# Block-sparse attention with a gated projection: the factor 0.125 moves from the queries to the maxima and the exponential

## The chip, the cores and the metric

The kernel runs on one core of one Trainium2 chip. The metric is device time in microseconds (us) of that core, the median of the runs. The engines are PE (TensorE: matmuls; PEld is its weight load), DVE (VectorE), ACT (ScalarE), POOL (GpSimd) and SP (SyncE, which here only issues DMAs). Each works through its own instructions in order; semaphores join them.

## The reference

What is computed, cut to what matters (batch B = 4, H = 8 heads, S = 768 rows, D = 64; blocks of 32 rows, 24 of them):

```python
scale = 1.0 / np.sqrt(D)                                  # 0.125
scores = scale * np.matmul(q, k.transpose(0, 1, 3, 2))
scores = np.where(mask, scores, -1000000000.0)
scores = scores - np.max(scores, axis=-1, keepdims=True)
attn = np.exp(scores)
attn = attn / (np.sum(attn, axis=-1, keepdims=True) + 1e-09)
x = np.matmul(attn, v)                                    # heads side by side: (B, S, 512)
gate = sigmoid(sum over k of conv_w[k] * x shifted by 4 - k rows)
out = (gate * (x @ w_val)) @ w_out
```

The mask lets a block see itself and its two neighbours, the first and the last block, and three sampled blocks; the first and last block see all and are seen by all. All data are fp32.

## The kernel before

The work goes in units. A *pair unit* is two neighbouring blocks of queries (64 rows) over all eight heads: each of its blocks has eight blocks of keys, 256 columns. A *global unit* holds queries of the first or last block, which see all 768 columns. Each batch has 11 pair units and 2 global ones, and there are 52 units in all. The 128 partitions of a score tile are 4 head pairs x 32 rows; the two heads of a head pair have a tile each, which is why most things happen twice per unit ("both heads").

For a unit, `scores` (from line 330) lets PE write the scores to PSUM (`sc`, three banks; `s` for global units). For each head DVE then takes the negated maxima (`mx`, line 365 for pairs: one reduce gives both blocks' maxima, 128 x 2). ACT takes the exponentials with the maximum as bias (`pe`, lines 367 and 368; `rest` and `first` in global units, lines 350 and 351). In a global unit two reduces per head give two partial maxima, and a small `tensor_tensor` joins them (line 348).

`transposes` turns the exponentials on PE (`pt`) and ACT copies them back to SBUF (`ptr`). `values` multiplies with the values (`av`); DVE forms the reciprocal of the sums (`rs`) and scales (`x`). `finish` transposes `x` into `xT`. Behind the attention comes the gated projection in rows of up to 384: DVE's convolution (`th`), ACT's splits (`xh`, `yh`), POOL's remainders (`xl`, `yl`), DVE's product (`y`) and two projections on PE (`vp`, `op`). In the first third DVE also decodes the two weight matrices from 64-bit words (`words`, `wst`, `wv`, `wo`).

The order on each engine is the order in which the program is written; the class `InOrder` (line 59) fixes it and is the reason why nearly every instruction has line 65 in the profile. The main loop (line 622) goes over steps n. In a step it issues the loads, the scores of unit n, the copies of keys (`kg`, on POOL and ACT in the first two batches, POOL and DMA later), the values of unit n - 2, the transposes of unit n - 1, and between them pieces of the projection (`fill`) and of decoding or gating (`prepare`).

Queries arrive by DMA in `qc` (128 x 256, five buffers). Before a unit's scores, `scale` (line 616) multiplies them in place by 0.125, two units ahead (`SCALE_AHEAD`): on ACT in batches 0 and 1, on DVE in batches 2 and 3, 24 times each.

Of the kernel before, what the change touches and what calls it, by code (L numbers as in the profile page):

```python
# [11 lines left out]
AF = mybir.ActivationFunctionType  # L12
ALU = mybir.AluOpType
# [19 lines left out]
LAG_T, LAG_V = 1, 2  # L33
WEIGHTS_AT = (1, 3, 5, 7, 9, 10, 11, 13)
DECODE_LAG = 2
SCALE_AHEAD = 2
COPY_AHEAD = 2

COPIED = [{0: POOL, 1: POOL, 2: POOL, 3: ACT, 4: ACT, 5: ACT}] * 2 + [{}] * 2
# [7 lines left out]
def attention_moe(ctx, tc, qb, kb, v, sampled, w_val, conv_w, w_out, ident_in, slot_in, out):  # L47
# [29 lines left out]
    pe, dve, act, pool, sp = (InOrder(e) for e in (nc.tensor, nc.vector, nc.scalar, nc.gpsimd, nc.sync))  # L77
# [45 lines left out]
    for r in range(NR):  # L123
# [3 lines left out]
            out=base[rows, :], in0=sf[rows, r, :], scalar1=float(BLK), scalar2=off[rows], op0=ALU.mult, op1=ALU.add  # L127
# [3 lines left out]
    def indices(b):  # L131

        row = const.tile([128, NB], F32, tag=f"row{b % 2}", name="row")
        dve.tensor_scalar_add(row, base, float(b * S - B * S))
        dve.tensor_tensor(out=row, in0=row, in1=valid, op=ALU.mult)
        dve.tensor_scalar_add(idx[:, b, :], row, float(B * S))
# [100 lines left out]
    for bt in batches:  # L237
        for p in [*range(GLOB_AFTER + 1), -1, *range(GLOB_AFTER + 1, NP - 1)]:
            pr = Pair()
# [4 lines left out]
    def block_numbers(pr, eng):  # L244

        mine = [n for n in range(2 * NR) if COPIED[pr.bt.b].get(n, SP) == eng]
        if not mine:
            return
        first = NR * PAIRS[pr.p][0] + mine[0]
        _, regs = nc.values_load_multi_w_load_instructions(  # L250
            sm[0:1, first : first + len(mine)], engines=[eng], min_val=0, max_val=NB - 1,
            skip_runtime_bounds_check_because="block numbers are drawn from [0, 24)",
        )
        for n, reg in zip(mine, regs):
            yield 5 + 4 * (n // NR) + n % NR, reg
# [69 lines left out]
    def heads():  # L325
        for hp in range(HP):
            for h in range(2):
                yield hp, h, slice(64 * h, 64 * h + 64), slice(BLK * hp, BLK * hp + BLK)

    def scores(un):  # L330
        pr = un.pr
        un.P = []
        if pr.glob:
            lo = [ps_sc.tile([128, 512], F32, tag="sc", name="s0") for _ in range(2)]
            hi = [space.tile([128, 512], F32, tag=tag, name="s1") for space, tag in ((ps_sc, "sc"), (ps_pt, "pt"))]
            for k0 in range(3):
                for hp, h, rows, cols in heads():
                    dst = hi[h][cols, 0:256] if k0 == 2 else lo[h][cols, 256 * k0 : 256 * k0 + 256]
                    matmul(
                        dst, pr.qc[rows, hp, un.e, :], pr.bt.k[rows, 8 * k0 : 8 * k0 + 8, cols],  # L340
                        start=True, stop=True, tile_position=(64 * h, BLK * hp),
                    )
            mx = three.tile([128, 2, 4], F32, tag="mx", name="mx")
            rest = five.tile([128, 2, 256], F32, tag="pr", name="rest")
            for h in range(2):
                dve.tensor_reduce(out=mx[:, h, 0:1], in_=lo[h], axis=AX.X, op=ALU.max, negate=True)
                dve.tensor_reduce(out=mx[:, h, 1:2], in_=hi[h][:, 0:256], axis=AX.X, op=ALU.max, negate=True)
                dve.tensor_tensor(out=mx[:, h, 2:3], in0=mx[:, h, 0:1], in1=mx[:, h, 1:2], op=ALU.min)
                first = five.tile([128, 512], F32, tag="pr", name="first")
                act.activation(rest[:, h, :], hi[h][:, 0:256], AF.Exp, bias=mx[:, h, 2:3])  # L350
                act.activation(first, lo[h], AF.Exp, bias=mx[:, h, 2:3])
                un.P.append(first)
            un.P.append(rest.rearrange("p h k -> p (h k)"))
            return
        sc = [ps_sc.tile([128, 2, 256], F32, tag="sc", name="sc") for _ in range(2)]
        kt = pr.kg.rearrange("p (t e) x -> p t e x", e=4)
        for j in range(2):
            for hp, h, rows, cols in heads():
                matmul(
                    sc[h][cols, j, :], pr.qc[rows, hp, j, :], kt[rows, 0 : 2 + j : 1 + j, :, cols],  # L360
                    start=True, stop=True, tile_position=(64 * h, BLK * hp),
                )
        mx = three.tile([128, 2, 4], F32, tag="mx", name="mx")
        for h in range(2):
            dve.tensor_reduce(out=mx[:, h, 0:2], in_=sc[h], axis=AX.X, op=ALU.max, negate=True)
            pe_ = five.tile([128, 2, 256], F32, tag="pr", name="pe")
            for j in range(2):
                act.activation(pe_[:, j, :], sc[h][:, j, :], AF.Exp, bias=mx[:, h, j : j + 1])
            un.P.append(pe_.rearrange("p j k -> p (j k)"))

    def transposes(un):
        un.PT = []
        for p in un.P:
            pt = ps_pt.tile([128, 4, 128], F32, tag="pt", name="pt")
            for c in range(4):
                transpose(pt[:, c, :], p[:, 128 * c : 128 * c + 128], ident)
            t = three.tile([128, 4, 128], F32, tag="ptr", name="ptr")
            act.copy(t, pt)
            un.PT += [t[:, c, :] for c in range(4)]
            yield  # L380
# [169 lines left out]
    def store():  # L550
        while stores:
            sp.dma_start(*stores.pop(0))
# [42 lines left out]
            advance(to_split, prepared)  # L595


    at = {"keys": 0, "values": 0, "copied": 0, "scaled": 0}
    N = len(units)

    def freed(k):

        return units[min(k, N - 1)].pr.seq if k >= 0 else -1

    def more(which, upto, load):
        if at[which] < len(pairs) and pairs[at[which]].seq <= upto:
            load(pairs[at[which]])
            at[which] += 1
            return True

    def until(which, n, do):
        while at[which] < min(len(pairs), pairs.index(units[min(n, N - 1)].pr) + 1):
            do(pairs[at[which]])
            at[which] += 1

    def scale(pr):
        if pr.bt.b < 2:
            act.activation(pr.qc, pr.qc, AF.Copy, scale=0.125)
        else:
            dve.tensor_scalar(out=pr.qc, in0=pr.qc, scalar1=0.125, scalar2=None, op0=ALU.mult)  # L620

    for n in range(N + LAG_V):
        step[0] = n

        def more_keys():
            return more("keys", freed(n - 1) + RING, load_keys)

        def more_values():
            return more("values", freed(n - LAG_V - 1) + VRING, load_values)

        if n == 0:
            more_keys()
            numbers_first = {eng: list(block_numbers(pairs[0], eng)) for eng in (POOL, ACT)}
            until("scaled", 0, scale)
            indices(0)
            until("copied", 0, copy_keys)
            more_keys()
            until("copied", 1, copy_keys)
            more_values()
        else:  # L640
            while more_keys() or more_values():
                more_values()
        until("scaled", n + (SCALE_AHEAD if n else 1), scale)
        store()
        k = len(staged)
        if k < 2 * CH and n >= WEIGHTS_AT[k] and (k < 4 or k - 4 in decoded):
            next(weights)

        if n < N:
            scores(units[n])  # L650
        if n == 0:
            more_keys()
        until("copied", n + COPY_AHEAD, copy_keys)
        if n == 0:
            while more_keys() or more_values():
                more_values()
        if 0 <= n - LAG_V < N:
            values(units[n - LAG_V])
        steps = STEPS_FIRST if n < FIRST else STEPS
        if 0 <= n - LAG_T < N:  # L660
            for half, _ in enumerate(transposes(units[n - LAG_T])):
                if not (half and n in HELD):
                    fill()
                prepare(steps)
        else:
            fill()
            prepare(steps)
        if 0 <= n - LAG_V < N and units[n - LAG_V].last:
            pr = units[n - LAG_V].pr
            finish(pr)  # L670
            pr.bt.done.add(pr.p)
            for t, (r0, rn) in enumerate(TILES[pr.bt.b]):
                need = {p for p in range(NP - 1) if any(r0 <= i * BLK < r0 + rn for i in PAIRS[p])}
                if r0 == 0 or r0 + rn == S:
                    need.add(-1)
                if t not in pr.bt.queued and need <= pr.bt.done:
                    pr.bt.queued.add(t)
                    queue_rows(pr.bt, t)
# [52 lines left out]
```

## Time and profile before

| | us |
|---|---|
| median of 3 runs | 411.16 |
| lowest, highest | 408.73, 413.2 |
| the profiled execution, its own time | 413.2 |
| its span, first to last instruction | 413.2 |
| DMA queues: bytes moved | 70.23 MB, 170 GB/s on average |

A line of the page or of a view names source line, engine, operation and tiles written and read. Busy time is a union over instructions of a group; "idle before" is the engine's idle time just in front of them, with what ended it. The chain of waits is followed back from the last instruction; an engine's share of it is time in which the end of the kernel hung on that engine. A duration of an instruction that another one overlaps counts in full in its own group.

### The profile page before, as it was taken

The numbers are of one execution on the slowest core, as the hardware profiler recorded it, in microseconds if no ns is written. First come the engines' busy times: TensorE is split into PE (matmuls) and PEld (weight loads), VectorE is DVE, ScalarE is ACT, GpSimd is POOL, SyncE is SP. The second block draws the span as 40 slices with busy tenths as digits, with TensorE's granted clock in tenths as the row PEclk, the third lists the DMA queues.
The fourth block names the chain that finished last, engine by engine and source line by source line (L and its number), as shares of the span: only waits on it lengthen the run. The fifth ranks groups of instructions, "written<-read, shape, count | busy, mean of one in ns | idle before, by whom it ended". The sixth has DMA issues, their size and how long they took to land.

```text
span 413.2 us, 16260 instructions
## 1 busy us (share of the span) xinstructions
PE 342.8 (83%) x6640; PEld 267.8 (65%) x6640; DVE 274.6 (66%) x601; ACT 263.3 (64%) x657; POOL 216.3 (52%) x318
## 2 busy tenths in 40 slices
PE   0873877777648999999779999989888899899993
PEld 0442555554335877787559878767756678688992
DVE  4445869899896974965783235985896247957620
ACT  2752778887677796768555656777566565864431
POOL 1864427748557167567634544767266254616240
PEclk9996899998897999999999999999999999999998
DMA  7897367788444245768876376569655563210210
GB/s 239 247 308 226 102 211 227 241 252 246 143 105 155 67 116 171 208 186 261 229 211 196 117 215 185 156 163 334 225 160 153 170 160 115 68 53 26 78 51 25
DMA packets 47522, 70.23 MB, mean 170 GB/s; under 512 B 6232, under 2 KB 29528, under 8 KB 47448
## 3 DMA queue, kind: packets, MB, share of 16 engines
q1 hardware_dynamic: 39976, 45.66, 36.2%
q0 software_dynamic: 7040, 23.43, 19.7%
q8 instruction: 52, 0.85, 0.8%
q14 instruction: 22, 0.18, 0.1%
q10 hardware_dynamic: 432, 0.11, 0.1%
HBM read 62.89 MB, written 6.29 MB: 167 GB/s over the span
## 4 chain that ended last, share of the span: by engine, by line
PE 35%; DVE 28%; DMA 17%; ACT 7%; issue 6%; POOL 3%; SPq 1%; ACTq 0%; POOLq 0%; DVEq 0%
PE vp L65 10%; DVE th L65 10%; PE op L65 9%; DVE mx L65 8%; PE av L65 6%; DMA va<-in_v 5%; PE pt L65 4%; DMA vn<-in_v 4%; PE sc L65 4%; DMA wst<-in_w_val 4%; DVE words L65 4%; ACT pe L65 2%; DVE wst L65 2%; DMA qc<-in_q 2%; POOL yl L65 2%
## 5 line engine op out<-in xcount | busy, mean ns | idle before, releaser
L65 POOL DMA_INDIRECT vb<-in_v,idx x88 | 88.9, 1010 | 82.6 <-PE av L65 49.0
L65 DVE SCALAR_TENSOR_TENSOR th<-xT,cw,th 128x384 f32<-128x384 f32 (+2 forms) x144 | 97.3, 687 | 14.7 <-ACT th L65 11.7
L65 ACT ACTIVATE pe<-sc,mx 128x256 f32<-128x256 f32 x176 | 69.1, 476 | 46.1 <-DVE mx L65 45.9
L65 DVE TENSOR_REDUCE mx<-sc 128x2 f32<-128x512 f32 x88 | 56.5, 683 | 60.5 <-PE sc L65 60.5
L65 PE MATMUL vp<-xh,wv 128*128 128x384 f32 (+2 forms) x288 | 74.7, 331 | 0.0
L65 ACT COPY ptr<-pt 128x512 f32<-128x512 f32 x112 | 64.8, 596 | 14.7 <-PE pt L65 14.4
L65 POOL TENSOR_TENSOR yl<-y,yh 128x384 fp32r<-128x384 f32 (+2 forms) x36 | 35.2, 978 | 71.2 <-ACT yh L65 71.0
L65 PE MATMUL op<-wo,yh 128*128 128x512 f32 x192 | 69.8, 410 | 0.7 <-issue 0.6
L65 PE MATMUL sc<-kg,qc 64*32 64x256 f32 x1408 | 53.4, 410 | 11.8 <-ACT kg L65 10.9
L65 POOL COPY kg<-k 128x256 f32<-128x256 f32 (+1 forms) x154 | 57.9, 414 | 8.7 <-DMA k<-in_k 8.5
L65 PE MATMUL pt<-ident,pe 128*128 128x128 f32 x352 | 54.6, 286 | 7.8 <-ACT rest L65 7.7
L65 PE MATMUL av<-va,ptr 128*32 128x65 f32 x1408 | 47.7, 230 | 10.8 <-DMA va<-in_v 8.1
L65 PEld LDWEIGHTS av<-va,ptr 128*32 128x32 f32 x1408 | 34.0, 114 | 30.8 <-issue 11.3
L65 PEld LDWEIGHTS vp<-xh,wv 128*128 128x128 f32 x288 | 50.8, 188 | 0.2 <-DVE y L65 0.2
L65 PEld LDWEIGHTS pt<-ident,pe 128*128 128x128 f32 x352 | 40.4, 144 | 16.1 <-ACT rest L65 8.8
L65 POOL TENSOR_TENSOR xl<-xT,xh 128x384 fp32r<-128x384 f32 (+2 forms) x36 | 35.2, 979 | 26.1 <-ACT xh L65 24.4
L65 PE MATMUL vp<-xl,wv 128*128 128x384 f32 (+2 forms) x144 | 46.5, 323 | 0.0
L65 PE MATMUL av<-vb,ptr 128*32 128x65 f32 x1408 | 46.4, 226 | 0.0
L65 PE MATMUL op<-wo,yl 128*128 128x512 f32 x96 | 38.3, 399 | 4.3 <-POOL yl L65 4.3
L65 PEld LDWEIGHTS sc<-kg,qc 64*32 64x32 f32 x1408 | 23.3, 111 | 27.2 <-POOL kg L65 12.0
L65 PEld LDWEIGHTS op<-wo,yh 128*128 128x128 f32 x192 | 36.1, 188 | 7.0 <-ACT yh L65 0.6
L65 PEld LDWEIGHTS av<-vb,ptr 128*32 128x32 f32 x1408 | 35.8, 114 | 0.0
(69 smaller groups left out, 449.0 us busy)
## 6 DMA issues: line engine op xcount, KB each, us to landing
kg<-in_k SPq DMA_DIRECT2D x132, 64.0 KB
va<-in_v SPq DMA_DIRECT2D x56, 130.0 KB
vn<-in_v SPq DMA_DIRECT2D x12, 520.0 KB
qc<-in_q SPq DMA_DIRECT2D x48, 128.0 KB
k<-in_k SPq DMA_DIRECT2D x12, 512.0 KB
out<-ot SPq DMA_DIRECT2D x24, 256.0 KB
wst<-in_w_val SPq DMA_DIRECT2D x4, 512.0 KB
wst<-in_w_out SPq DMA_DIRECT2D x4, 512.0 KB
```

What stands on the lines that cost most here:

```text
L65: made = getattr(self.eng, name)(*args, **kwargs)
```

## The change

Queries are no longer scaled. The scores are therefore eight times larger, and so are their negated maxima. The exponential computes exp(0.125 * score + bias), for which the bias must be 0.125 times the negated maximum. In pair units a new `tensor_scalar` on DVE multiplies the two maxima by 0.125 into columns 2 and 3 of `mx`, once per head. In global units the joining `tensor_tensor` becomes a `tensor_scalar` that takes the minimum with a column operand and multiplies by 0.125 in the same instruction. `scale`, `SCALE_AHEAD` and the two calls in the main loop go.

```diff
-SCALE_AHEAD = 2
+SCALE = 0.125
...
             for h in range(2):
                 dve.tensor_reduce(out=mx[:, h, 0:1], in_=lo[h], axis=AX.X, op=ALU.max, negate=True)
                 dve.tensor_reduce(out=mx[:, h, 1:2], in_=hi[h][:, 0:256], axis=AX.X, op=ALU.max, negate=True)
-                dve.tensor_tensor(out=mx[:, h, 2:3], in0=mx[:, h, 0:1], in1=mx[:, h, 1:2], op=ALU.min)
+                dve.tensor_scalar(
+                    out=mx[:, h, 2:3], in0=mx[:, h, 0:1], scalar1=mx[:, h, 1:2], scalar2=SCALE, op0=ALU.min, op1=ALU.mult
+                )
                 first = five.tile([128, 512], F32, tag="pr", name="first")
-                act.activation(rest[:, h, :], hi[h][:, 0:256], AF.Exp, bias=mx[:, h, 2:3])
-                act.activation(first, lo[h], AF.Exp, bias=mx[:, h, 2:3])
+                act.activation(rest[:, h, :], hi[h][:, 0:256], AF.Exp, bias=mx[:, h, 2:3], scale=SCALE)
+                act.activation(first, lo[h], AF.Exp, bias=mx[:, h, 2:3], scale=SCALE)
...
         for h in range(2):
             dve.tensor_reduce(out=mx[:, h, 0:2], in_=sc[h], axis=AX.X, op=ALU.max, negate=True)
+            dve.tensor_scalar(out=mx[:, h, 2:4], in0=mx[:, h, 0:2], scalar1=SCALE, scalar2=None, op0=ALU.mult)
             pe_ = five.tile([128, 2, 256], F32, tag="pr", name="pe")
             for j in range(2):
-                act.activation(pe_[:, j, :], sc[h][:, j, :], AF.Exp, bias=mx[:, h, j : j + 1])
+                act.activation(pe_[:, j, :], sc[h][:, j, :], AF.Exp, bias=mx[:, h, 2 + j : 3 + j], scale=SCALE)
...
-    def scale(pr):
-        if pr.bt.b < 2:
-            act.activation(pr.qc, pr.qc, AF.Copy, scale=0.125)
-        else:
-            dve.tensor_scalar(out=pr.qc, in0=pr.qc, scalar1=0.125, scalar2=None, op0=ALU.mult)
...
-            until("scaled", 0, scale)
...
-        until("scaled", n + (SCALE_AHEAD if n else 1), scale)
```

On PE, POOL and SP no instruction comes, goes or changes places. On DVE 88 come, 24 go and 16 change their kind; on ACT 24 go. At three places this reads as follows (a row is line, operation, tiles and shape; "x2" stands for two alike in a row).

On DVE, in batch 0 while the first weight matrix is decoded, before:

```order
L65 TENSOR_SCALAR wst<-words 128x512
L65 SCALAR_TENSOR_TENSOR wv_130<-wst 128x512
L65 TENSOR_REDUCE mx<-sc 128x2 x2
L65 TENSOR_SCALAR rs<-av 128x4
L65 RECIPROCAL rs<-rs 128x4
```

and now:

```order
L65 TENSOR_SCALAR wst<-words 128x512
L65 SCALAR_TENSOR_TENSOR wv_130<-wst 128x512
L65 TENSOR_REDUCE mx<-sc 128x2
L65 TENSOR_SCALAR mx<-mx 128x2
L65 TENSOR_REDUCE mx<-sc 128x2
L65 TENSOR_SCALAR mx<-mx 128x2
L65 TENSOR_SCALAR rs<-av 128x4
L65 RECIPROCAL rs<-rs 128x4
```

The second head's reduce and all that follows on DVE now stand behind a scaling that waits for the reduce in front of it.

On DVE, in batch 2 or 3, where the queries' scaling stood between the gating work and the maxima, the difference is:

```order
 L65 SCALAR_TENSOR_TENSOR th<-xT,cw,th 128x384 x6
-L65 TENSOR_SCALAR qc<-qc 128x256
-L65 TENSOR_REDUCE mx<-sc 128x2 x2
+L65 TENSOR_REDUCE mx<-sc 128x2
+L65 TENSOR_SCALAR mx<-mx 128x2
+L65 TENSOR_REDUCE mx<-sc 128x2
+L65 TENSOR_SCALAR mx<-mx 128x2
 L65 TENSOR_SCALAR rs<-av 128x4
 L65 RECIPROCAL rs<-rs 128x4
```

One operation of 256 columns went, two of 2 columns came.

On ACT, in batch 0, in front of a pair unit's exponentials:

```order
 L65 CAST wv_129<-words 128x512
 L65 COPY ptr<-pt 128x512 x2
-L65 ACTIVATE qc<-qc 128x256
 L65 ACTIVATE pe<-sc,mx 128x256 x4
 L250 TENSOR_LOAD sm
```

The scaling of a later unit's queries no longer stands ahead of the exponentials.

More of the change, by code (lines that the diff above doesn't have):

```diff
@@ L595, in prepare @@
             advance(to_split, prepared)
-    at = {"keys": 0, "values": 0, "copied": 0, "scaled": 0}
+    at = {"keys": 0, "values": 0, "copied": 0}
     N = len(units)
```

## The prediction

> **What bounds the kernel now.** I read the page first: spans, busy shares, and the chain of work that ended last.
>
> ```profile
> span 413.2 us, 16260 instructions
> PE 342.8 (83%) x6640; PEld 267.8 (65%) x6640; DVE 274.6 (66%) x601; ACT 263.3 (64%) x657; POOL 216.3 (52%) x318
> PE 35%; DVE 28%; DMA 17%; ACT 7%; issue 6%; POOL 3%; SPq 1%; ACTq 0%; POOLq 0%; DVEq 0%
> ```
>
> No engine bounds the whole span. PE is busiest, yet the chain spends almost as much time on DVE (VectorE). So the next view is the busy time by stage (columns: length, then busy time of PE, PEld, DVE, ACT, POOL, then the granted TensorE clock, DMA share and GB/s).
>
> ```profile
> 36.00:110.00 74.00, 49.86 (x1396) 34.92 (x1396) 65.83 (x140) 55.44 (x152) 42.73 (x75) 0.93 0.69 213
> 165.00:310.00 145.00, 134.46 (x2474) 108.13 (x2477) 97.53 (x211) 95.77 (x220) 81.97 (x98) 1.00 0.69 203
> 360.00:413.30 53.30, 46.47 (x388) 40.86 (x387) 25.93 (x55) 22.28 (x57) 17.16 (x23) 0.97 0.13 49
> ```
>
> From 36 to 110 us DVE is busy 89% of the time (65.83 of 74): the weights are decoded there between the maxima. Later PE is (134.46 of 145, 93%). After 360 us no scores are left, and the change touches nothing. The chain in order of time tells which maxima lie on the path (start, length, what; "mx" is the maxima, "x2" both heads):
>
> ```profile
> 52.76 0.69 DVE mx L65
> ...
> 62.17 1.28 DVE mx L65 x2
> 63.45 0.08 DVE rs L65
> ...
> 166.16 0.20 DVE qc L65
> ...
> 251.81 0.70 DVE mx L65
> 252.54 0.80 ACT pe L65 x2
> ...
> 259.48 0.41 DVE qc L65
> ...
> 275.13 1.20 DVE mx L65 x2
> ...
> 311.36 0.30 DVE qc L65
> ...
> 350.39 0.61 DVE mx L65
> ```
>
> The chain takes the maxima in two ways. With both heads (DVE's own order is the path; `rs` follows on DVE) it does so 13 times, first at 62.17, last at 275.13. With one head, leaving to the exponentials on ACT (ScalarE), it does so 7 times, first at 52.76, last at 350.39. Five more passes are global units.
>
> **The change, part by part.**
>
> *The new scaling of the maxima, 88 of them.* Nearest rows: the small DVE operation that already follows a reduce, and other small ones (min/median/max ns).
>
> ```profile
> L65 DVE TENSOR_TENSOR mx<-mx x16: 159/160/1647, 39.3 to 313.9; 128x1 f32<-128x1 f32 x16
> L65 DVE TENSOR_SCALAR rs<-av x48: 142/153/164, 21.7 to 368.7; 128x4 f32<-128x4 f32 x48
> L65 DVE TENSOR_SCALAR row<-base x4: 170/172/178, 9.3 to 274.3; 128x24 f32<-128x24 f32 x4
> L65 DVE TENSOR_REDUCE mx<-sc x88: 670/682/693, 12.9 to 358.4; 128x2 f32<-128x512 f32 x88
> ```
>
> So 142 to 178 ns by itself; I take 160, the row with the same place in the order. What it adds to DVE is more subtle, since neighbours overlap. In the timeline (start, length):
>
> ```profile
> 12.93 1.29 DVE L65 TENSOR_REDUCE mx<-sc 128x2 f32<-128x512 f32 x2 [2.99 <-PE sc L65]
> 13.66 1.57 ACT L65 ACTIVATE pe<-sc,mx 128x256 f32<-128x256 f32 x4 [1.49 <-DVE mx L65]
> ...
> 38.23 1.01 DVE L65 TENSOR_REDUCE mx<-s 128x1 f32<-128x512 f32 x2
> 39.28 0.16 DVE L65 TENSOR_TENSOR mx<-mx 128x1 f32<-128x1 f32 x1
> 39.35 1.02 DVE L65 TENSOR_REDUCE mx<-s 128x1 f32<-128x512 f32 x2
> ```
>
> Two reduces of 0.68 end after 1.29, so the second starts 0.61 after the first. The dependent operation starts 0.04 after the reduce's end (38.23 + 1.01 = 39.24), and the next reduce 0.07 after that start. With one in between, reduce to reduce is 0.68 + 0.04 + 0.07 = 0.79: +0.18 us of DVE each, +0.36 per pair of heads. For the exponential of the first head the delay is 0.04 + 0.16 = 0.20. On the path: 13 x 0.36 = 4.7, 7 x 0.20 = 1.4, together +6.1 us. The other units cost nothing on the path: there DVE idles before the maxima and later work covers them. Were that cover gone, all 88 would cost 88 x 0.18 = 15.8.
>
> *The wait that it adds.* The second head's reduce, and whatever DVE has next (`rs`, decoding, gating), queues behind it; ACT's exponentials wait for it, and behind them ACT's copies of the transposes and keys. Those are counted where they lie on the path. The scores stay in PSUM 0.2 to 0.4 us longer, and PE may wait for that bank:
>
> ```profile
> L65 PE MATMUL sc<-kg,qc 64*32 64x256 f32 x1408 | 53.4, 410 | 11.8 <-ACT kg L65 10.9 <-ACT pe L65 0.9
> ```
>
> It waited there for exponentials 0.9 us in the whole run, so I take 0, at worst that size again.
>
> *The shared port.* A reduce reads PSUM and writes SBUF; the new operation reads and writes SBUF, like others that this trace shows being held up while POOL (GpSimd) works:
>
> ```profile
> 119.77 1.44 POOL L65 COPY kg<-k 128x256 f32<-128x256 f32 x5
> 120.53 1.65 DVE L65 TENSOR_TENSOR mx<-mx 128x1 f32<-128x1 f32 x1
> 121.18 0.98 POOL L65 TENSOR_TENSOR xl<-xT,xh 128x384 fp32r<-128x384 f32 x1
> ```
>
> By tile (min/median/max ns), and by group (busy us, mean ns of one, idle before):
>
> ```profile
> L65 DVE TENSOR_SCALAR qc<-qc x24: 280/302/489, 166.1 to 338.3; 128x256 f32<-128x256 f32 x24
> L65 DVE SCALAR_TENSOR_TENSOR y<-th,vp x36: 286/544/556, 140.7 to 404.0; 128x384 f32<-128x384 f32 x28, 128x256 f32<-128x256 f32 x4, 128x128 f32<-128x128 f32 x4
> ...
> L65 DVE TENSOR_TENSOR mx<-mx 128x1 f32<-128x1 f32 x16 | 6.1, 378 | 0.5
> L65 DVE TENSOR_SCALAR qc<-qc 128x256 f32<-128x256 f32 x24 | 8.2, 342 | 0.0
> ```
>
> The operation at 120.53 ended at 122.18, where POOL's ended at 122.16. `y`, with one input in PSUM, never exceeds 556. Bounds: 0 per operation (as `y`), or 378 - 160 = 0.218 us (as the minimum of two SBUF columns). I take 342 - 280 = 0.06, rounded up to 0.07, because `qc` is the same kind of operation. On the path stand 2 x 13 + 7 = 33: +2.3 us, between 0 and 7.2.
>
> The Trainium skill, "SBUF — State Buffer", section "Who interferes with whom", has a rule that speaks against this change: a tensor_scalar in SBUF can enter a two-port mode and is then shut out for the whole of a GpSimd instruction, while a tensor_reduce never is. By the wait at 120.53 the trace agrees on the lock; no row here is a two-element tensor_scalar. By the rule the term may lie anywhere up to the 7.2 above; with no lock it is 0 and the sum +3.7 us.
>
> *Global units: tensor_tensor becomes tensor_scalar with a column operand, 16.* Row for such operands:
>
> ```profile
> L65 DVE TENSOR_SCALAR base<-sf,slot x3: 221/221/230, 8.4 to 9.1; 32x24 f32<-32x24 f32 x3
> ```
>
> 221 against 172 for `row`, +0.05; ten of the 16 are on the path: +0.5 us. In return the new form may escape the port: lateness in all is 16 x 0.218 = 3.5 us, most of it at 120.53 and in other global units on the path. Ends: 0 (still held) and -3.5. Neither `y` (one SBUF tensor, never held) nor `qc` (held at times) is nearer, and a wait removed from the path saves only down to the next path, so I take -1.4.
>
> *Removed: 24 scalings of queries on ACT and 24 on DVE.*
>
> ```profile
> L65 ACT ACTIVATE qc<-qc 128x256 f32<-128x256 f32 x24 | 10.2, 429 | 6.0 <-DMA qc<-in_q 6.0
> ...
> ACT pe L65 <- DVE mx L65: 45.9, 42, 2.2
> ```
>
> ACT's 10.2 us appear nowhere on the chain; ACT sat idle 45.9 us before the exponentials until the maxima were there, and that wait, which the change lengthens, hides them. Price 0. DVE's 8.2 us are on the path only where a queue of gating work runs into the maxima: six pieces, from 0.20 at 166.16 over 0.41 at 259.48 to 0.30 at 311.36, 1.5 us in sum: -1.5 us. No other queue moves; DMAs are the same.
>
> *The factor inside the exponential.* ACT's copies of 512 elements with and without a factor:
>
> ```profile
> L65 ACT ACTIVATE ot<-op x24: 595/603/643, 161.3 to 406.8; 128x512 f32<-128x512 f32 x24
> L65 ACT COPY ptr<-pt x112: 571/590/627, 19.7 to 366.0; 128x512 f32<-128x512 f32 x112
> ```
>
> At most 13 ns apart; for 7 passes with up to four exponentials that is under 0.4 us. I take 0.
>
> Sum: 6.1 + 2.3 + 0.5 - 1.4 - 1.5 = +6.0 us. The profiled execution took 413.2 us, all of it inside its span, and is the slowest of the three shown; the sum gives it 419.2. Against the median of 411.16 that is 417.2 us.
>
> **The rivals.** About 1% is what a measurement of this kernel can tell from no change: 4.1 us, so the lines are 407.0 and 415.3.
>
> *Small (no measurable change).* The port never holds the new operation (0 for 2.3) and frees the global ones fully (-3.5 for -1.4): 6.1 + 0.5 - 3.5 - 1.5 = +1.6 us, 412.8. For it: `y` at 556 at most. Against: `qc`, the same kind of operation, is at times held.
>
> *Heavy port.* Each new operation is held as the old minimum was: 33 x 0.218 = 7.2, and no relief: 6.1 + 7.2 + 0.5 - 1.5 = +12.3 us, 423.5. For it: POOL's key copies run near the maxima, as at 119.77. Against: `qc`. By the Trainium skill ("SBUF — State Buffer", "Who interferes with whom") every POOL instruction can do this, and the time would be this rival's.
>
> *ACT was the hidden bound (faster).* Between 36 and 165 us ACT sheds 18 scalings:
>
> ```profile
> 36.00:110.00 74.00, 16.45 (x432) 7.17 (x432) 0.00 (x0) 4.81 (x11) 0.93 0.69 213
> 110.00:165.00 55.00, 10.30 (x256) 4.00 (x256) 0.00 (x0) 2.97 (x7) 0.91 0.40 116
> ```
>
> (the fourth busy figure is ACT's, for operations on `qc`): 4.81 + 2.97 = 7.8 us. If ACT's order released every step there, the gain would be 7.8, the DVE additions in that stretch would vanish behind it, and 411.2 - 7.8 = 403.4. It decides once ACT, not DVE, ends the steps' last wait; ACT's 55.44 busy against DVE's 65.83, and ACT's idle waits for the maxima, speak against it.
>
> **How the numbers follow.** Forecast as summed, 0.50; small 0.28; heavy port 0.16; ACT 0.06. The forecast's own range is 413.5 to 421. From the small case's 412.8 and the heavy one's 423.5, with a microsecond or so for neighbours that shift, the range is 411.5 to 423.5. Faster by over 1%: the ACT rival, 0.06. Within 1%: the small case and the forecast's low end, 0.28 + 0.06 = 0.34. Slower by over 1%: 0.44 of the forecast and the heavy case, 0.60.
>
> **What would show it.** In the changed profile: 88 `mx<-mx` operations of about 160 ns median, with a mean telling the port's share (0.07 above is my guess, 0.2 the heavy case); reduce to reduce 0.79 instead of 0.61; DVE's share of the chain up by some 6 us and no new ACT entries; the global `mx<-mx` near 210 ns with no value over a microsecond if the relief is real. ACT's wait for the maxima grows beyond 45.9 us. Wrong would be a chain on which the passes through the maxima become fewer, which means that the added time fell into slack that I did not see.

## The result and the profile after

The changed kernel takes 425.62 us (median of five runs, 422.18 to 427.38) against 411.16 before (five runs, 408.73 to 413.2). The ratio is 1.0376, with a 95% interval of 1.0312 to 1.044: slower by some 15 us. Ratios, here and below, are estimates from the fast runs alone, without those in a slower state that the chip shows at times, and need not be the quotients of the medians beside them (1.035 here). The direction was forecast, the size was not: 417.2 us was forecast, with a range that ended at 423.5.

The two profiled executions make the difference look smaller. Before's took 413.2 us, the slowest of its runs, and the one of after took 422.18, the fastest. Their spans are 413.2 and 420.2 us. So the traces tell where the time goes, and the timed ratios how much it is.

The page of after, the lines that answer to those of before (busy time by engine; the chain by engine; the chain by line), and last the chain by line of the page of before:

```profile
span 420.2 us, 16393 instructions
PE 347.8 (83%) x6640; PEld 271.0 (65%) x6640; DVE 289.6 (69%) x665; ACT 258.2 (61%) x633; POOL 214.5 (51%) x318
PE 38%; DVE 34%; ACT 9%; DMA 8%; issue 5%; POOL 2%; SPq 2%; ACTq 0%; DVEq 0%; POOLq 0%
DVE mx L65 15%; DVE th L65 11%; PE vp L65 10%; PE op L65 10%; PE sc L65 6%; PE av L65 5%; PE pt L65 5%; DMA wst<-in_w_val 4%; DVE words L65 3%; DMA va<-in_v 3%; ACT pe L65 2%; ACT ptr L65 2%; DVE x L65 2%; SPq L65 1%; PE s L65 1%
...
PE vp L65 10%; DVE th L65 10%; PE op L65 9%; DVE mx L65 8%; PE av L65 6%; DMA va<-in_v 5%; PE pt L65 4%; DMA vn<-in_v 4%; PE sc L65 4%; DMA wst<-in_w_val 4%; DVE words L65 4%; ACT pe L65 2%; DVE wst L65 2%; DMA qc<-in_q 2%; POOL yl L65 2%
```

The maxima have 15% of the chain, 63 us of 420; summed over the chain of before they had 34.8 us. ACT is less busy by 5 us, yet the kernel is slower. The groups of small operations on the maxima, kept apart by shape (busy us, mean ns | idle before), and by tile (min/median/max ns):

```profile
L65 DVE TENSOR_SCALAR mx<-mx 128x2 f32<-128x2 f32 x88 | 28.7, 326 | 3.0
L65 DVE TENSOR_SCALAR mx<-mx 128x1 f32<-128x1 f32 x16 | 3.4, 214 | 0.6
...
L65 DVE TENSOR_SCALAR mx<-mx x104: 168/169/2199, 13.7 to 366.9; 128x2 f32<-128x2 f32 x88, 128x1 f32<-128x1 f32 x16
```

The 88 new operations take 168 ns at the least and half of them at most 169, yet 326 on average. So a few are very late: 88 x (326 - 168) = 13.9 us in all. One by one, 23 of the 88 are more than 20 ns over the minimum. In their first 168 ns, 13 of the 23 meet a copy or a subtraction of POOL and ten meet an indirect load of POOL. Of the 65 others, 35 meet no POOL instruction, 29 meet an indirect load and one meets a copy. The 16 operations of the global units are all at 214 ns, and none is late.

One place shows both the size and the shape of it. In the timeline of after (start, length, instruction) this is a pair unit near 155 us:

```profile
154.50 0.69 DVE L65 TENSOR_REDUCE mx<-sc 128x2 f32<-128x512 f32 x1 [1.02 <-PE sc L65]
154.96 1.46 POOL L65 COPY kg<-k 128x256 f32<-128x256 f32 x5
155.23 0.57 DVE L65 TENSOR_SCALAR mx<-mx 128x2 f32<-128x2 f32 x1
155.71 0.68 DVE L65 TENSOR_REDUCE mx<-sc 128x2 f32<-128x512 f32 x1
155.89 0.84 ACT L65 ACTIVATE pe<-sc,mx 128x256 f32<-128x256 f32 x2 [1.84 <-DVE mx L65]
156.39 1.00 POOL L65 TENSOR_TENSOR yl<-y,yh 128x384 fp32r<-128x384 f32 x1
156.42 1.96 DVE L65 TENSOR_SCALAR mx<-mx 128x2 f32<-128x2 f32 x1
157.36 1.00 POOL L65 TENSOR_TENSOR xl<-xT,xh 128x384 fp32r<-128x384 f32 x1
```

The first scaling (155.23) meets POOL's key copies and takes 0.57 us. The second starts 0.03 after POOL's subtraction `yl` and ends at 158.38, when the next one, `xl`, ends at 158.36: it waited for both. The first reduce to the end of the second scaling is 3.88 us; the two reduces alone took 1.29 before. The chain of after runs straight through it (start, length):

```profile
154.52 0.68 DVE mx L65
155.21 0.02 issue
155.23 1.17 DVE mx L65 x2
156.40 0.02 issue
156.42 1.96 DVE mx L65
158.38 0.07 DVE rs L65
158.46 0.02 issue
158.48 0.47 ACT pe L65
```

The chain goes through 48 of the 88 operations. Among these are 17 of the 23 late ones, with 10.6 of the 13.9 us of lateness.

### The profile page after: what moved, and what is told of

Same layout as the page of the kernel before. It is cut to its first block, busy times and chain, and to the rows that moved or that the text cites. A ratio compares the mean times of both kernels' runs of the same rounds, so it can differ in the third digit from the quotient of the medians.

```text
span 420.2 us, 16393 instructions
## 1 busy us (share of the span) xinstructions
PE 347.8 (83%) x6640; PEld 271.0 (65%) x6640; DVE 289.6 (69%) x665; ACT 258.2 (61%) x633; POOL 214.5 (51%) x318
## 4 chain that ended last, share of the span: by engine, by line
PE 38%; DVE 34%; ACT 9%; DMA 8%; issue 5%; POOL 2%; SPq 2%; ACTq 0%; DVEq 0%; POOLq 0%
DVE mx L65 15%; DVE th L65 11%; PE vp L65 10%; PE op L65 10%; PE sc L65 6%; PE av L65 5%; PE pt L65 5%; DMA wst<-in_w_val 4%; DVE words L65 3%; DMA va<-in_v 3%; ACT pe L65 2%; ACT ptr L65 2%; DVE x L65 2%; SPq L65 1%; PE s L65 1%
## 5 line engine op out<-in xcount | busy, mean ns | idle before, releaser
L65 POOL DMA_INDIRECT vb<-in_v,idx x88 | 87.8, 997 | 81.3 <-PE av L65 46.9
L65 ACT ACTIVATE pe<-sc,mx 128x256 f32<-128x256 f32 x176 | 72.0, 471 | 71.5 <-DVE mx L65 51.2
L65 DVE TENSOR_REDUCE mx<-sc 128x2 f32<-128x512 f32 x88 | 60.2, 684 | 60.3 <-PE sc L65 57.9
L65 PE MATMUL op<-wo,yh 128*128 128x512 f32 x192 | 70.7, 415 | 3.1 <-ACT yh L65 2.4
L65 PE MATMUL pt<-ident,pe 128*128 128x128 f32 x352 | 55.6, 291 | 5.7 <-ACT rest L65 5.7
L65 PEld LDWEIGHTS pt<-ident,pe 128*128 128x128 f32 x352 | 41.5, 147 | 13.7 <-ACT rest L65 6.2
L65 PEld LDWEIGHTS av<-va,ptr 128*32 128x32 f32 x1408 | 32.8, 113 | 22.3 <-ACT ptr L65 8.2
L65 PEld LDWEIGHTS sc<-kg,qc 64*32 64x32 f32 x1408 | 24.6, 111 | 27.0 <-POOL kg L65 11.8
L65 PEld LDWEIGHTS av<-vb,ptr 128*32 128x32 f32 x1408 | 34.7, 114 | 1.6 <-issue 1.6
```

The source lines that it names most:

```text
L65: made = getattr(self.eng, name)(*args, **kwargs)
```

## The experiments

All ratios are against the kernel before, run beside it on the same chip. On the first chip used here before took 410.95 us, on the later ones 420.15 and 419.07, so only ratios are compared across chips. Two theories were set against each other for the loss: *port*, that the new operations are held up while POOL works, and *order*, that they cost by their mere place between maximum and exponential. A third, *removal*, was that the loss comes from taking the query scaling away.

**Without the 88 operations.**

```diff
-            dve.tensor_scalar(out=mx[:, h, 2:4], in0=mx[:, h, 0:2], scalar1=SCALE, scalar2=None, op0=ALU.mult)
...
-                act.activation(pe_[:, j, :], sc[h][:, j, :], AF.Exp, bias=mx[:, h, 2 + j : 3 + j], scale=SCALE)
+                act.activation(pe_[:, j, :], sc[h][:, j, :], AF.Exp, bias=mx[:, h, j : j + 1], scale=SCALE)
```

> The changed kernel without its 88 new operations in the pair units; everything else of the change stays. Leaves out: the maxima of pair units are not multiplied by 0.125, so the exponential's bias is the full negated maximum. Theory port (the new operations cost mostly by being held while POOL works) and rival order (they cost by standing on DVE in front of the exponentials, 0.18 to 0.20 us each, held or not) both expect the loss to vanish: 0.985 to 1.000 of before, 405 to 411 us, since DVE's 1.5 us of query scaling on the path and up to 3.5 us of held minima in global units are gone as well. Rival removal (taking the query scaling away shifts work so that the kernel gets slower by itself) expects 1.01 or more, 415 us and up.

Measured: 410.88 us, ratio 0.9997 (0.9955 to 1.0038). The loss is gone, so it all hangs on the 88 operations, and *removal* falls. But nothing is gained either: 48 scalings of queries fewer, the factor in every exponential and the new form in the global units come to zero together.

**The 88 operations alone, on the kernel before.**

```diff
             dve.tensor_reduce(out=mx[:, h, 0:2], in_=sc[h], axis=AX.X, op=ALU.max, negate=True)
+            dve.tensor_scalar(out=mx[:, h, 2:4], in0=mx[:, h, 0:2], scalar1=1.0, scalar2=None, op0=ALU.mult)
...
-                act.activation(pe_[:, j, :], sc[h][:, j, :], AF.Exp, bias=mx[:, h, j : j + 1])
+                act.activation(pe_[:, j, :], sc[h][:, j, :], AF.Exp, bias=mx[:, h, 2 + j : 3 + j])
```

> The kernel before, with its query scaling, plus the 88 operations alone (a multiplication of the pair units' maxima by 1.0, the same instruction at the same place). Port and order: at least the change's loss, since nothing is taken away: 1.035 to 1.045 of before, 426 to 430 us. Removal: within 1% of before. Lateness of the new operations as in the changed kernel: some 20 to 25 of 88 held, 14 us in sum, and the old global minima held again.

Measured: 430.53 us, ratio 1.0476 (1.0404 to 1.0547). The operations alone cost as much as the whole change, or a little more; the intervals of the two overlap. By tile:

```profile
L65 DVE TENSOR_SCALAR mx<-mx x88: 168/170/2678, 13.9 to 376.6; 128x2 f32<-128x2 f32 x88
```

As expected, 20 of the 88 are late, by 14.7 us in sum, and the old form in the global units is late again, up to 1385 ns.

**A second reduce in their place.**

```diff
-            dve.tensor_scalar(out=mx[:, h, 2:4], in0=mx[:, h, 0:2], scalar1=SCALE, scalar2=None, op0=ALU.mult)
+            dve.tensor_reduce(
+                out=mx[:, h, 2:4], in_=mx[:, h, 0:2].rearrange("p (a o) -> p a o", o=1), axis=AX.X, op=ALU.max
+            )
```

> The changed kernel with each of the 88 multiplications replaced by a second tensor_reduce over an axis of length one, 128x2 to 128x2 in SBUF, same place and same waits. Leaves out: the factor 0.125 on the maxima of pair units. Port: reduces are not held in any row so far, so lateness falls from 13.9 us to about 0 and the time to 1.00 to 1.02 of before, 411 to 419 us (what is left is 13 x 0.36 + 7 x 0.20 = 6.1 us on the path less 1.5 and less 3.5). Order: no difference to the changed kernel, 1.03 to 1.04, 423 to 427 us.

Measured: 415.07 us, ratio 1.0143 (1.0094 to 1.0192). The groups by shape of this run, and the new operation by tile:

```profile
L65 DVE TENSOR_REDUCE mx<-mx 128x2 f32<-128x2 f32 x88 | 13.6, 155 | 3.0
L65 DVE TENSOR_SCALAR mx<-mx 128x1 f32<-128x1 f32 x16 | 3.4, 214 | 0.6
...
L65 DVE TENSOR_REDUCE mx<-mx x88: 154/155/159, 13.7 to 359.9; 128x2 f32<-128x2 f32 x88
```

The same number of operations of the same shape, at the same place with the same waits, take 155 ns each, all between 154 and 159. They met POOL no less: 18 of the 88 met a copy or a subtraction in their first moments, and none was late. More than half of the loss is gone with the lateness. That is *port*; what *order* leaves is 1.43%, or 1.46% over the run without operations, 6.0 us.

**The changed kernel and the second reduce on one chip.** The measurement of the changed kernel itself had been on a chip of its own, so the pair was run together, with no edit beyond that of the second reduce.

> The changed kernel as it is, on one chip with the run after it, since the earlier ones ran on several. Port: 1.03 to 1.045 of before, with 20 to 25 of the 88 operations late, 12 to 17 us in sum. Rival (the gap between the changed kernel and the second reduce came from different chips): 1.015 to 1.025.

> The second reduce in place of the 88 multiplications once more (the factor on the maxima of pair units is left out), on the same chip as the changed kernel. Port: 1.01 to 1.02 of before and 2 to 2.5% below the changed kernel, no lateness. Rival (chips): within 1% of the changed kernel.

Measured: 434.45 us, ratio 1.0345 (1.0301 to 1.0388), and 424.6 us, ratio 1.012 (1.0073 to 1.0167). The gap is 9.85 us, 2.3%, as it had been across chips. The groups of the first:

```profile
L65 DVE TENSOR_SCALAR mx<-mx 128x2 f32<-128x2 f32 x88 | 28.4, 322 | 3.0
```

It is 322 ns on average here with a minimum of 169, so 88 x 0.153 = 13.5 us late in all, and 21 of 88 late by over 20 ns. The second reduce had 155 again.

**Two operations of one column instead of one of two.**

```diff
-            dve.tensor_scalar(out=mx[:, h, 2:4], in0=mx[:, h, 0:2], scalar1=SCALE, scalar2=None, op0=ALU.mult)
+            for j in range(2):
+                dve.tensor_scalar(
+                    out=mx[:, h, 2 + j : 3 + j], in0=mx[:, h, j : j + 1], scalar1=SCALE, scalar2=None, op0=ALU.mult
+                )
```

> The changed kernel with each 128x2 multiplication split into two of 128x1; it computes the reference. The 128x1 form with a column operand in the global units was never late (213 to 215 ns, 16 times). Port, if a one-element form is never held: lateness about 0, but twice the operations: 0.18 us more on DVE per head than the reduce in place of it, 33 x 0.18 = 6 us on the path above that run, 1.015 to 1.03 of before, 417 to 424 us. Port, if the one-element form without a column operand is held too: late ones as in the changed kernel and 1.045 or more, 430 us. Order: 33 x 0.18 = 6 us above the changed kernel, 1.045 to 1.055, 430 to 434 us.

Measured: 417.12 us, ratio 1.0183 (1.0139 to 1.0227). By tile:

```profile
L65 DVE TENSOR_SCALAR mx<-mx x192: 143/153/216, 13.7 to 362.9; 128x1 f32<-128x1 f32 x192
```

Of 192 operations none exceeds 216 ns, and that is the time of the 16 with a column operand. Of the 176 others, 42 met a copy or a subtraction of POOL in the same way. This is the same kind of operation on the same tile, twice as many of them, and the kernel is 1.6 to 1.9% faster than with the 88 of two columns (1.0345 and 1.0376). The doubled count was expected to cost 6 us over the second reduce; it cost 2.05 us on the same chip, and the intervals of the two overlap. What costs most is not the count but whether the form was held.

**The multiplication on ACT.**

```diff
-            dve.tensor_scalar(out=mx[:, h, 2:4], in0=mx[:, h, 0:2], scalar1=SCALE, scalar2=None, op0=ALU.mult)
+            act.activation(mx[:, h, 2:4], mx[:, h, 0:2], AF.Copy, scale=SCALE)
```

> The changed kernel with the 88 multiplications of the maxima on ACT instead of DVE (one 128x2 copy with the factor 0.125 per head, just in front of its exponentials); it computes the reference. Port: ACT's operations were never held in any run, and DVE's order is that of the run without the operations; what is left is some 0.2 us in front of a head's exponentials where the path runs through them (7 passes in the trace of before, 1.4 us) and 88 x 0.2 = 18 us more on ACT in total, mostly in its waits: 1.000 to 1.012 of before, 411 to 416 us. Rival (any small operation between maximum and exponential costs its place, wherever it runs): as with the second reduce or more, 1.014 to 1.02, 417 to 419 us.

Measured: 424.06 us, ratio 1.0119 (1.0061 to 1.0177), at the upper edge of the one expectation, with an interval that reaches into the rival's. By tile, and the first unit in the timeline:

```profile
L65 ACT ACTIVATE mx<-mx x88: 200/203/220, 15.9 to 366.6; 128x2 f32<-128x2 f32 x88
...
15.20 1.29 DVE L65 TENSOR_REDUCE mx<-sc 128x2 f32<-128x512 f32 x2 [4.41 <-PE sc L65]
15.93 0.20 ACT L65 ACTIVATE mx<-mx 128x2 f32<-128x2 f32 x1 [3.11 <-issue]
16.16 0.84 ACT L65 ACTIVATE pe<-sc,mx 128x256 f32<-128x256 f32 x2
```

None is late, and DVE has nothing to do for it: its two reduces take 1.29 again. The exponential starts 0.96 after the reduce, and 0.73 before the change. Still 1.2% is lost, almost as much as with the second reduce on DVE. Either the delay of 0.2 us in front of each head's exponentials costs that, or the 88 x 0.203 = 17.9 us of new work on ACT does; no run tells the two apart.

**One multiplication for both heads, after the second reduce.**

```diff
-            dve.tensor_scalar(out=mx[:, h, 2:4], in0=mx[:, h, 0:2], scalar1=SCALE, scalar2=None, op0=ALU.mult)
+        dve.tensor_scalar(out=mx[:, :, 2:4], in0=mx[:, :, 0:2], scalar1=SCALE, scalar2=None, op0=ALU.mult)
+        for h in range(2):
             pe_ = five.tile([128, 2, 256], F32, tag="pr", name="pe")
```

> The changed kernel with one multiplication for both heads after the second reduce (128x2x2) instead of one per head: 44 operations instead of 88; it computes the reference. Port: half the operations, so about half the lateness (7 us for 13.9) and half the place (0.18 once per pair on 13 passes, 2.3 us), but the first head's exponentials start 0.6 us later on the 7 single passes, 4 us: 1.015 to 1.03 of before, 417 to 424 us. Rival (lateness goes by how long POOL's stretches are, not by how often DVE asks, so one asker meets nearly as much): 1.03 to 1.04.

Measured: 433.5 us, ratio 1.0352 (1.0291 to 1.0412), as slow as the change. The ratio is the rival's, but its reason is not: the lateness did fall.

```profile
L65 DVE TENSOR_SCALAR mx<-mx 128x4 f32<-128x4 f32 x44 | 12.3, 279 | 1.5
...
14.34 1.29 DVE L65 TENSOR_REDUCE mx<-sc 128x2 f32<-128x512 f32 x2 [4.08 <-PE sc L65]
15.66 0.23 DVE L65 TENSOR_SCALAR mx<-mx 128x4 f32<-128x4 f32 x1
15.99 1.57 ACT L65 ACTIVATE pe<-sc,mx 128x256 f32<-128x256 f32 x4 [3.99 <-DVE words L65]
```

With a minimum of 169, 44 x (279 - 169) = 4.8 us are late, a third of the change's. But the first exponential now starts 1.65 us after the first reduce, against 0.73 before and 0.96 with ACT's multiplication. It is so throughout: the median over the 44 pair units is 1.59 us here, 0.72 before, 0.96 with ACT's multiplication and 0.99 in the changed kernel. The first expectation had priced the later start at seven places; if it is the cause, it costs at many more. That it is the cause is argued from these starts, not shown by a run of its own.

**The global units' part alone, and with it all query scaling on ACT.** Both on the kernel before; the second has both edits.

```diff
-                dve.tensor_tensor(out=mx[:, h, 2:3], in0=mx[:, h, 0:1], in1=mx[:, h, 1:2], op=ALU.min)
+                dve.tensor_scalar(
+                    out=mx[:, h, 2:3], in0=mx[:, h, 0:1], scalar1=mx[:, h, 1:2], scalar2=1.0, op0=ALU.min, op1=ALU.mult
+                )
...
-        if pr.bt.b < 2:
-            act.activation(pr.qc, pr.qc, AF.Copy, scale=0.125)
-        else:
-            dve.tensor_scalar(out=pr.qc, in0=pr.qc, scalar1=0.125, scalar2=None, op0=ALU.mult)
+        act.activation(pr.qc, pr.qc, AF.Copy, scale=0.125)
```

> The kernel before with the global units' part of the change alone: the joining tensor_tensor becomes a tensor_scalar with a column operand (times 1.0); queries are scaled as before. Port: the 3.5 us of lateness of the old form go, 16 x 0.05 us come back, and as most of it lay on the path: 0.990 to 0.997 of before, 407 to 410 us. Rival (what is saved there falls into the next path, and the run without operations came out even because nothing in the change gains): 0.998 to 1.003.

> As the run with the global part alone, and the query scaling of batches 2 and 3 moves from DVE to ACT, so that no query scaling is left on DVE. Port and path: DVE loses 24 operations, 8.2 us busy, 1.5 us on the path and 1.5 us of lateness, ACT gains 24 x 0.43 = 10 us in its waits: 0.985 to 0.997 of before, 405 to 410 us. Rival (ACT in batches 2 and 3 has no room, so the exponentials wait): 1.00 to 1.02.

Measured: 417.53 us, ratio 0.9971 (0.9928 to 1.0014), and 417.41 us, ratio 0.995 (0.9914 to 0.9987). By itself the new form in the global units can't be told from no change. With the query scaling off DVE as well, the kernel is 0.5% below before, about 2 us, and the interval excludes 1 by little. Against the global part alone the step is 0.2%, well inside both intervals. So a gain over before is not established; the lead over the changed kernel is. Of the 16 operations none took more than 215 ns in either run.

## Why the prediction was wrong, point by point

*The place of the 88 operations: +6.1 us forecast.* The second reduce against the run without operations gives 1.0143 / 0.9997, 1.46%, 6.0 us, with some 2.6 us either way by the two intervals. The size held. The minimum was 168 ns for the 160 taken, and from reduce to reduce it was 0.80 us in the median of the 44 pair units, for the 0.79 taken. Whether the division held is doubtful: 4.7 of the 6.1 were put on DVE's own order and 1.4 on the start of the exponentials. ACT's multiplication, which leaves DVE alone, costs 1.0119 / 0.9997, 1.2%, 5.0 us. If that is the later start, it counts in more than the seven passes, and the sum of chain passes came out right partly by luck; if it is ACT's new work, the division may stand.

*The shared port: +2.3 us forecast.* This is the step that failed: the term for the shared port was mis-sized, at 2.3 us for a measured 9.85 (changed kernel less second reduce on one chip, with some 2.7 us either way). The mechanism was named, and the runs bear it out. Both factors of the term were too small. The mean lateness was taken as 0.07 us, from the scaling of queries ("because `qc` is the same kind of operation"); it was 0.158. The row that I passed over as an upper bound, the old minimum at the same place in the order, had 0.218; neither row gave the size. And lateness was charged at 33 of the 88 places, as if it fell evenly; in fact 23 operations hold all of it, up to 2 us each, and the chain of after goes through 48 places, with 17 of these 23. Three quarters of the lateness (10.6 of 13.9 us) ended on the chain, and about as much of it, 9.85 us, in the time. That long waits put their places on the path is a reading of this chain: six late ones, such as that of 1.75 us at 276.09, stayed off it.

That POOL is what they wait for is read from the traces, where each late one meets a POOL instruction; no run took POOL's work away. The form is shown by runs: at the same place the reduce and the one-column multiplication met POOL's copies and subtractions and were never late.

*Global units: +0.5 and -1.4.* 0.9971 is -1.2 us of 420.15 where -0.9 was forecast, inside the noise. The column operand costs 214 ns against the forecast 210, and the relief is real in the operations themselves: no value over 216 in any run with the new form, where before one took 1647. In the time it can't be told from nothing.

*Removed scaling: -1.5 us forecast.* Not found. The run without the operations has both this and the global part, and stands at 0.9997. Nor do ACT's 10.2 us show in it. The rival in which ACT was the hidden bound, 403.4 us or 0.981, lies outside the interval of the same run. The sign that the prediction named for ACT, a wait for the maxima above 45.9 us, tells nothing: it is 51.2 us in the changed kernel and 51.9 in the run without the operations.

*The factor inside the exponential: 0.* It held: the median of `pe` is 473 ns after and 475 before. (The two rows from which it was taken are 13 ns apart in the median, but 24 at the minimum, not "at most 13".)

*The rivals.* The heavy port (423.5 us, 0.16) is the nearest to what happened, and even that was short. It took 7.2 us for the port, which measured 9.85, and it did so with a lateness that was too large, 0.218 for 0.158, at too few places. Its other half, no relief in the global units, did not come true. The range ended at this rival's sum, with nothing added above it. Summed from the runs, 6.0 + 9.85 - 0.1 = 15.8 us on before, a ratio of 1.038 for the measured 1.0376; since the terms are differences between the same kernels, that shows only that the chips agree.

The Trainium skill, "SBUF — State Buffer", section "Who interferes with whom", lets a tensor_scalar in SBUF that runs in a two-port mode be shut out by a whole GpSimd instruction and a tensor_reduce never. The runs agree on both: 88 multiplications up to 2.2 us, 88 reduces at 159 ns at most. They go beyond it in the extent: the operation at 156.42 waited for two GpSimd instructions back to back, 1.96 us.

Left open: why the scaling of queries was never more than 0.21 us late in the trace of before, while the same kind of operation behind a reduce was up to 2 us late. Its place in the step does not explain it, for it met the same POOL instructions. In the timeline of before:

```profile
187.73 1.01 POOL L65 TENSOR_TENSOR yl<-y,yh 128x384 fp32r<-128x384 f32 x1 [0.94 <-ACT yh L65]
188.41 0.49 DVE L65 TENSOR_SCALAR qc<-qc 128x256 f32<-128x256 f32 x1
188.70 1.06 POOL L65 TENSOR_TENSOR xl<-xT,xh 128x384 fp32r<-128x384 f32 x1
```

It began during `yl` and ended at 188.90, long before `xl` did: it went in between the two. So it did at such a place in two other runs, 0.36 us late (the global part alone) and 0.62 us late (the 88 operations alone), where the operation of two columns waited for both three times.

## What to carry to other kernels

A tiny operation is priced by what it can wait for, not by its 0.17 us: before one is put between a reduce and its consumer, look at which form other operations have that are late while another engine works, and let the range reach past the latest of the nearest rows. Here neither the row of the same kind (0.06 us late) nor the one at the same place (0.218) gave the 0.158 that was measured, and the places on the chain of before were too few. If it must stand there, choose a form that was never late: here two multiplications of one column cost 1.8% where one of two columns cost 3.5 to 3.8%. Work that hides in an engine's waits, as the query scaling did here, need not bring a gain when it is removed.

## What the runs showed that was not expected

The form decided, not the amount of work. A multiplication of 128x2 was late 23 times in 88, up to 2.2 us, while that of 128x1 was late in none of 192, whether its factor was a constant (143 to 155 ns) or came with a column operand (212 to 216 ns). A late operation often did not go in between two POOL instructions that follow each other: it went through `yl` and `xl` together three times (1.96, 1.92 and 2.20 us). Of the ten late ones that began over an indirect load of POOL, five met nothing else and were 0.12 to 0.23 us late; in the five others a copy or a subtraction followed the load, and the wait was 0.16 to 2.03 us. The 29 others that met a load were on time.
